# Input loads ordered tensor by tensor, weight quarters between them, two scalars loaded late, and a new list order for a gated linear attention with an MLP behind it

## The chip, the cores and the metric

The kernel runs on one core of one Trainium2 chip. The metric is the device time of one execution in microseconds (us), lower is better. TensorE (PE) multiplies matrices, VectorE (DVE) and ScalarE (ACT) work on elements, GpSimd (POOL) does a few products and casts, SyncE (SP) only issues DMAs here. Each engine takes its own instructions strictly in the order in which they were written; semaphores join the engines.

## The reference, cut to what matters

A linear attention whose state decays by `alpha` feeds a two-layer MLP with a squared relu:

```python
# q, k, v, alpha: (4 batches, 8 heads, 768 steps, 48); w_in (384, 2048), w_out (2048, 384)
for t in range(S):
    state = alpha[:, :, t, :, None] * state + einsum('bhd,bhe->bhde', k[:, :, t], v[:, :, t])
    y[:, :, t] = einsum('bhd,bhde->bhe', q[:, :, t], state)
x = y.transpose(0, 2, 1, 3).reshape(B * S, H * D)      # 3072 tokens of 384
r = maximum(x @ w_in, 0)
out = (s * (r * r) + b) @ w_out                         # s and b are single numbers
```

The kernel computes the attention in chunks. With c the running sum of log(alpha) in a chunk it forms q·exp(c) and k·exp(-c), multiplies them, masks the product to the lower triangle and multiplies it by v; what came before the chunk enters through the state.

## The kernel before

**Blocks.** The 3072 tokens are 24 blocks of 128, six to a batch. Blocks are numbered from 0. A block needs four loads of 192 KB (`a` for alpha, `q`, `k`, `v`), each into one of five buffers of its kind (`NIN = 5`). Then, per block:

- `ln` (ACT) takes the logarithm, `cum` (PE) sums it with a triangular matrix, `ei` and `eb` (ACT) take exp(-c), exp(c) and the decay over the block.
- `kb` and `qb` (DVE) multiply k and q by these; `vc` (POOL) casts v to bf16.
- q and k are transposed: in blocks below `NPE` by eight PE transposes (`T`) and a DVE copy (`Tc`), in the others by a DMA transpose that ACT issues (`Td`).
- `KV` (PE) forms the block's share of the state, `t1` (DVE) adds the old state, `sn` (POOL) applies the decay.
- `A` (PE, L404) multiplies k by q, `mk` (DVE, L413) masks, `y` (PE, L442) multiplies by v and adds the old state, `ye` (ACT, L466) copies y to bf16. From block `NAY` on, `A` of a block and `y` of the block before it are one unit of PE work, `st_Ay`; below it they are two.

**MLP.** Two blocks form a group (12 groups). A group takes eight *units* of `mm1` (L488, six matmuls of 128x256: two of the 16 slices of `w_in`), each followed by `re` (relu, ACT, L497) and `sq` (two squares, DVE, L505). It then takes eight *quads* of `mm2` (L512, four matmuls of 128x384; four quads make a block's output row), and `oe` (DVE, L523) scales by s, adds the bias and writes the tile that `ostore` (SP, L535) stores. Units and quads are counted from 0 to 95 each. Quad 4c+3 ends output c.

**Weights.** `w_in` and `w_out` come in quarters of 768 KB (`i0` to `i3`, `o0` to `o3`) through four staging buffers. ACT casts each to bf16 (`ci`, `co`; L250, L263). DVE also sums the `w_out` quarters over rows (`cp`, `ca`; L271, L276). The bias row is b times that sum: `bias_mul` (DVE, L279) makes a matrix full of b, `bias_mm` (PE, L285) multiplies it by the sums, `bias_copy` (DVE, L294) brings it to SBUF.

**What sets the order.** All of this is written down as a list of operations for a list scheduler (`Schedule`), which runs when the program is built. Each operation has an engine, a planned duration, a priority and the names it reads and writes. Per engine the scheduler takes, among the operations that could begin first by its plan, the one with the lowest priority number. The order in which it starts them is the order in which the instructions are written for each engine. Operations marked `lock` do not overlap with each other in the plan (DVE and POOL). A block's priorities are `want(n)` plus an offset in `P`; `UNIT`, `LEAD`, `P_BM`, `P_CS`, `P_BMM` and `NAY`, `NPE` shape them. `LOADS` lists the loads on SP: the scheduler sees them with priorities around -1000, so SP issues them as soon as a buffer is free, in the list's order, while stores have -2000. In the kernel before, `LOADS` holds whole blocks (`b1` means `a1 q1 k1 v1`), with the eight weight quarters between them; block 0 is issued ahead of the list, and `b` and `s` (512 bytes each after the broadcast to 128 partitions) are issued by ACT at the start. Before the first quad PE fills planned idle time with small matmuls on zeros (`fill`, L674).

Of the kernel before, what the change touches and what calls it, by code (L numbers as in the profile page):

```python
# [15 lines left out]
VW = 144  # L16

GROUPS = [2, 2, 2, 2, 2, 2, 2, 2, 2, 2, 2, 2]
UNIT = 1.396
LEAD = {1: 72.9, 2: 87.9, 4: 83.9}  # L20

NPE = 9

NAY = 5

RING = 12

NST = 4

TB = 1.1  # L30
TW = 2.3
FILL_GAP = 0.45

P_BM, P_CS, P_BMM = -5, -48.2, -221.5
P = dict(
    ln=9.85, cum=-2.97, eb=3.53, ei=-4.54, vc=-2.78, qb=15.79, kb=-10.16, T=5.42,
    Tc=-1.09, KV=4.4, t1=4.97, sn=-0.59, Ay=-5.51, A=-4.02, mk=-10.39, y=12.28,
    ye=-10.99, m1=3.02, re=-4.95, sq=-1.4, m2=14.39, oe=-25.12,
)

LOADS = ["b0", "i0", "i1", "b1", "i2", "b2", "b3", "i3", "o0", "o1", "o2", "o3", "b4", "b5", "b6"]

class Schedule:
    HOP = 0.05
# [6 lines left out]
    def op(self, eng, dur, prio, fn, *args, r=(), w=(), lat=0.08, lock=False):  # L51
        me = len(self.ops)
        deps = set()
        for x in r:
            if x in self.writer:
                deps.add(self.writer[x])
        for x in w:
            if x in self.writer:
                deps.add(self.writer[x])
            deps.update(self.readers.get(x, ()))  # L60
        for x in r:
            self.readers.setdefault(x, []).append(me)
        for x in w:
            self.writer[x] = me
            self.readers[x] = []
        self.ops.append((eng, dur, prio, fn, args, deps, lat, lock))
# [67 lines left out]
def kernel(  # L134
# [12 lines left out]
    nc = tc.nc  # L147
# [6 lines left out]
    NBLK = B * NCH  # L154
# [3 lines left out]
    NIN = 5  # L158
# [16 lines left out]
    def many(name, n, shape, dtype, zero=None):  # L175
        tiles = []
        for i in range(n):
            t = sb.tile(shape, dtype, name=f"{name}{i}")
            if zero is not None:
                zero.memset(t, 0.0)  # L180
            tiles.append(t)
        return tiles


    a_in = many("a_in", NIN, [128, H, D], FP32)
    q_in = many("q_in", NIN, [128, H, D], FP32)
    k_in = many("k_in", NIN, [128, H, D], FP32)
    v_in = many("v_in", NIN, [128, H, D], FP32)
    s_col = sb.tile([128, 1], FP32, name="s_col")
    b_col = sb.tile([128, 1], FP32, name="b_col")  # L190
# [8 lines left out]
    for src, dst in ((alpha, a_in), (q, q_in), (k, k_in), (v, v_in)):  # L199
        load(0, src, dst)  # L200
    nc.scalar.preload_act_table_set("natural_log_exp_and_others")
    nc.scalar.dma_start(out=b_col, in_=moe_b.to_broadcast((128, 1)))
    nc.scalar.dma_start(out=s_col, in_=moe_s.to_broadcast((128, 1)))

    la_sb = many("la", 2, [128, H, 64], BF16, zero=nc.vector)
    U_bf = sb.tile([128, 128], BF16, name="U_bf")
# [29 lines left out]
    bones = sb.tile([128, 128], FP32, name="bones")  # L236
# [37 lines left out]

    def colsum_add():
        nc.vector.tensor_tensor(out=colsum, in0=colsum, in1=colpart, op=ALU.add)  # L276

    def bias_mul():
        nc.vector.tensor_scalar(  # L279
            out=bones, in0=ones_f, scalar1=b_col, scalar2=None, op0=ALU.mult  # L280
        )
# [257 lines left out]
    op = sched.op  # L539
    NG = len(GROUPS)  # L540

    def first(n):
        return n % NCH == 0

    def last(n):
        return n % NCH == NCH - 1

    def want(n):
        g, t = blk_group[n]
        return (4 * n - LEAD[GROUPS[g]]) * UNIT  # L550

    loads = LOADS + [f"b{n}" for n in range(NBLK) if f"b{n}" not in LOADS]
    stage = 0
    for rank, item in enumerate(loads):
        t, i = rank - 1000, int(item[1:])
        if item[0] == "b":
            if i == 0:
                for x, name in enumerate("aqkv"):
                    op("SP", 1.4 if x == 0 else 0.85, t + 0.01 * x, lambda: None,
                       w=[(name, 0)], lat=2.0)  # L560
                op("DVE", 0.3, P_BM, bias_mul, w=["bones"], lock=True)
            continue
        st = stage % NST
        stage += 1
        if item[0] == "i":
            op("SP", TW, t, load_w_in, i, st, w=[("wst", st)], lat=2.0)
            op("ACT", 1.4, -500, cast_w_in, i, st, r=[("wst", st)], w=[("wib", i)])
        else:
            op("SP", TW, t, load_w_out, i, st, w=[("wst", st)], lat=2.0)
            op("ACT", 1.4, -400, cast_w_out, i, st, r=[("wst", st)], w=[("wob", i)])  # L570
            op("DVE", 0.88, P_CS, colsum_part, i, st, r=[("wst", st)],
               w=["colpart" if i else "colsum"], lock=True)
            if i:
                op("DVE", 0.88, P_CS, colsum_add, r=["colpart"], w=["colsum"], lock=True)
# [5 lines left out]
    def yevac_op(n):  # L580
        g = blk_group[n][0]
        op("ACT", 0.41, want(n) + P["ye"], st_yevac, n, r=["py"], w=[("xd", g % 3, blk_group[n][1])])
# [3 lines left out]
    def add_block(n):  # L586
        i2, i3, ii = n % 2, n % 3, n % NIN
        t = want(n)
        if n:
            rank = loads.index(f"b{n}") - 1000  # L590
            for x, (name, src, dst) in enumerate(
                (("a", alpha, a_in), ("q", q, q_in), ("k", k, k_in), ("v", v, v_in))
            ):
                op("SP", TB, rank + 0.1 * x, load, n, src, dst, w=[(name, ii)], lat=2.0)
        op("ACT", 0.45, t + P["ln"], st_ln, n, r=[("a", ii)], w=[("la", i2)])
        op("PE", 0.27, t + P["cum"], st_cum, n, r=[("la", i2)], w=["ct"], lat=0.16)
        op("ACT", 0.41, t + P["eb"], st_exp_b, n, r=["ct"], w=[("b", i2)])
        op("ACT", 0.49, t + P["ei"], st_exp_i, n, r=["ct"], w=[("bi", i2), ("bl", i2)])
        op("POOL", 0.5, t + P["vc"], st_vcast, n, r=[("v", ii)], w=[("vp", n % 4)], lock=True)
        op("DVE", 0.48, t + P["qb"], st_qb, n, r=[("q", ii), ("b", i2)], w=[("qb", i3)], lock=True)  # L600
        op("DVE", 0.48, t + P["kb"], st_kb, n, r=[("k", ii), ("bi", i2)], w=[("kb", i3)], lock=True)
        if n < NPE:
            op("PE", 0.45, t + P["T"], st_T, n, r=[("qb", i3), ("kb", i3)], w=["ct"], lat=0.16)
            op("DVE", 0.61, t + P["Tc"], st_Tcopy, n, r=["ct"], w=[("qkT", i3)])
        else:
            op("ACT", 1.25, t + P["T"], st_Tdma, n, r=[("qb", i3), ("kb", i3)],
               w=[("tq", i3), ("qkT", i3)], lat=0.1)
            op("SP", 1.95, -3000, lambda: None, r=[("tq", i3)], w=[("qkT", i3)], lat=2.0)
        op("PE", 0.17, t + P["KV"], st_KV, n, r=[("kb", i3), ("vp", n % 4)], w=["py"], lat=0.16)
        if first(n):  # L610
            op("DVE", 0.65, t + P["t1"], st_t1, n, r=["py", ("bl", i2)], w=[("S", i3)])
        elif not last(n):
            op("DVE", 0.65, t + P["t1"], st_t1, n, r=["py", ("S", (n - 1) % 3)], w=[("t1", i2)])
            op("POOL", 0.85, t + P["sn"], st_snew, n, r=[("t1", i2), ("bl", i2)], w=[("S", i3)], lock=True)
        rA, wA = [("qkT", i3)], ["a"]
        late = n + 1 < NBLK and n + 1 >= NAY
        if n >= NAY:
            r1, w1 = ys.pop(n - 1)
            op("PE", 0.935, want(n - 1) + P["Ay"], st_Ay, n, r=rA + r1, w=wA + w1, lat=0.16)
            yevac_op(n - 1)  # L620
        else:
            op("PE", 0.43, t + P["A"], st_A, n, r=rA, w=wA, lat=0.16)
        op("DVE", 1.14, t + P["mk"], st_mask, n, r=["a"], w=[("am", i2)])
        rr = [("am", i2), ("qkT", i3), ("vp", n % 4)] + ([] if first(n) else [("S", (n - 1) % 3)])
        if late:
            ys[n] = (rr, ["py"])
        else:
            op("PE", 0.6, t + P["y"], st_y, n, r=rr, w=["py"], lat=0.16)
            yevac_op(n)

    def add_group(g):
# [4 lines left out]
        for u in range(NJ // per):  # L636
            w = unit_i
            unit_i += 1
            js = units[w][1]
            t = w * UNIT  # L640
            op("PE", 0.85 if m == 1 else 0.65, t + P["m1"], mm1, w,
# [5 lines left out]
        for u in range(4 * m):  # L647
# [3 lines left out]
            ob = (x // 4) % 2  # L651
            t = (x + 4 * m + P["m2"]) * UNIT
            op("PE", 0.65, t, mm2, x,
# [7 lines left out]
    for n in range(NBLK):  # L661
        add_block(n)

        if n and n >= NAY and blk_group[n - 1][0] != blk_group[n][0]:
            add_group(blk_group[n - 1][0])
        if (n + 1 < NAY or n + 1 == NBLK) and n + 1 == first_blk[blk_group[n][0]] + GROUPS[blk_group[n][0]]:
            add_group(blk_group[n][0])
# [41 lines left out]
```

## Time and profile before

| what | value |
| --- | --- |
| median of 5 runs | 199.25 us (197.66 to 200.53) |
| the profiled execution's own time | 198.28 us |
| its span, first to last instruction | 196.2 us |
| TensorE clock granted in it | 1.000 |
| PE, DVE, ACT, POOL busy | 176.5, 148.1, 108.8, 33.9 us |
| loads and stores | 34.16 MB moved, 174 GB/s mean |
| filler matmuls (L674) | 58, 10.6 us |

The span leaves out 2.1 us of the execution's time that lie around the first and last instruction. Durations come from the one profiled execution. A busy PE counts filler matmuls and matmuls whose ends are modelled, so busy time is not the same as work done. Where matmuls follow one another without a gap, the time from one start to the next is the better measure: 0.65 us for a unit of `mm1` or a quad of `mm2`, 0.33 for `A`, 0.51 for `y` (0.34 in the first block of a batch), 0.27 for `cum`, 0.19 for `KV`, 0.46 for eight transposes.

### The profile page before, as it was taken

Reading aid. Unit: us, or ns where it says so; the run is one execution under the profiler, and the core shown is the slowest. Engines: PE = TensorE matmul, PEld = TensorE weight load, DVE = VectorE, ACT = ScalarE, POOL = GpSimd, SP = SyncE. Lnnn points to the kernel's source line nnn. Section 1 sums busy time; section 2 is a strip of 40 time slices with the busy share of each in tenths; the row PEclk is TensorE's granted clock in tenths of the full one; section 3 lists DMA queues with packets and bytes.
Section 4 is the critical chain, followed back from the end, with each engine's and each line's share of the span. In section 5 each row is a group of like instructions: output and inputs, shape, how many; then the busy total and the mean of one; then the engine's idle time right before and its main releaser. Section 6 shows DMA issues by size and latency. Waiting matters only on the chain.

```text
span 196.2 us, 5398 instructions
## 1 busy us (share of the span) xinstructions
PE 176.5 (90%) x2126; PEld 127.5 (65%) x2126; DVE 148.1 (75%) x353; ACT 108.8 (55%) x225; POOL 33.9 (17%) x60
## 2 busy tenths in 40 slices
PE   0688988599999899999999699999999999999992
PEld 0456766367567567777777477677676677776861
DVE  4344697799988999798977878857898889775541
ACT  3172974995235666557566467267467257355520
POOL 8401321001202123120121220301130221100000
PEclk9999999999999999999999999999999999999999
DMA  4999899977999989996699985999697899510012
GB/s 83 251 291 256 173 234 380 327 141 164 192 186 227 199 167 173 204 216 133 143 195 143 202 185 119 191 241 181 138 240 145 169 198 178 97 40 24 19 40 82
DMA packets 123161, 34.16 MB, mean 174 GB/s; under 512 B 116480, under 2 KB 121600, under 8 KB 123136
## 3 DMA queue, kind: packets, MB, share of 16 engines
q1 hardware_dynamic: 107008, 29.89, 68.9%
q10 hardware_dynamic: 16128, 3.94, 12.4%
q8 instruction: 16, 0.26, 0.6%
q14 instruction: 9, 0.07, 0.1%
HBM read 25.17 MB, written 4.72 MB: 152 GB/s over the span
## 4 chain that ended last, share of the span: by engine, by line
PE 60%; DMA 17%; DVE 15%; issue 3%; ACT 1%; SPq 1%; ACTq 0%; DVEq 0%
PE o_ps L512 24%; PE h_ps L488 22%; DMA k_in<-in_k_dram 8%; DMA wst<-in_moe_w_out_dram 5%; PE py_ps L442 4%; DVE gt L505 4%; DMA qkT<-qk 4%; PE a_ps L404 3%; DVE am L413 2%; DVE qkT L371 2%; PE o_ps L674 2%; PE ct_ps L348 2%; PE ct_ps L304 1%; DVE t L387 1%; DVE colpart L271 1%
## 5 line engine op out<-in xcount | busy, mean ns | idle before, releaser
L497 ACT ACTIVATE r<-h_ps 128x512 bf16<-128x512 f32 x96 | 55.8, 600 | 34.6 <-PE h_ps L488 19.2
L512 PE MATMUL o_ps<-w_out_bf,gt 128*128 128x384 bf16 x384 | 71.8, 326 | 2.6 <-ACT w_out_bf L263 2.6
L488 PE MATMUL h_ps<-xd,w_in_bf 128*128 128x256 bf16 x576 | 72.5, 273 | 0.6 <-ACT xd L466 0.2
L505 DVE TENSOR_TENSOR gt<-r 128x256 bf16<-128x256 bf16 x192 | 55.6, 337 | 15.7 <-ACT r L497 15.1
L488 PEld LDWEIGHTS <-w_in_bf 128*128 128x128 bf16 x576 | 54.6, 98 | 10.9 <-issue 1.2
L512 PEld LDWEIGHTS <-gt 128*128 128x128 bf16 x384 | 35.8, 98 | 22.2 <-issue 2.7
L413 DVE TENSOR_TENSOR am<-a_ps,mask 128x1024 bf16<-128x1024 f32 x24 | 29.3, 1219 | 2.0 <-PE a_ps L404 1.7
L398 POOL TENSOR_TENSOR s_st<-t,blast 128x384 bf16<-128x384 bf16 x16 | 14.6, 912 | 65.5 <-DVE t L387 37.9
L325 POOL CAST vp<-v_in 128x384 bf16<-128x384 f32 x24 | 13.9, 578 | 67.4 <-DMA v_in<-in_v_dram 53.0
L466 ACT ACTIVATE xd<-py_ps 128x384 bf16<-128x384 f32 x24 | 11.8, 490 | 22.6 <-PE py_ps L442 21.0
L523 DVE SCALAR_TENSOR_TENSOR o_sb<-o_ps,s_col,bias_w 128x384 f32<-128x384 f32 x24 | 14.8, 616 | 7.3 <-PE o_ps L512 6.5
L336 DVE TENSOR_TENSOR qk<-k_in,binv 128x384 bf16<-128x384 f32 x24 | 13.8, 577 | 8.6 <-ACT binv L321 6.5
L298 ACT ACTIVATE la<-a_in 128x384 bf16<-128x384 f32 x24 | 12.5, 522 | 5.4 <-DMA a_in<-in_alpha_dram 3.7
L321 ACT ACTIVATE binv<-ct_ps 128x384 f32<-128x384 f32 x24 | 11.8, 491 | 4.6 <-PE ct_ps L309 4.4
L331 DVE TENSOR_TENSOR qk<-q_in,b_s 128x384 bf16<-128x384 f32 x24 | 13.5, 563 | 0.3
L404 PE MATMUL a_ps<-qkT 64*128 64x128 bf16 x192 | 9.7, 222 | 4.1 <-DVE qkT L371 2.4
L318 ACT ACTIVATE b_s<-ct_ps 128x384 f32<-128x384 f32 x24 | 12.1, 505 | 1.5 <-issue 1.5
L387 DVE TENSOR_TENSOR t<-py_ps,s_st 64x192 bf16<-64x192 f32 x32 | 11.3, 353 | 2.1 <-PE py_ps L362 1.7
L304 PE MATMUL ct_ps<-la,U_bf 128*128 128x384 bf16 x24 | 8.0, 335 | 4.9 <-ACT la L298 4.8
L404 PEld LDWEIGHTS <-qkT 64*128 64x128 bf16 x192 | 5.5, 95 | 10.6 <-DVE qkT L371 4.5
L442 PE MATMUL py_ps<-am,vp 128*32 128x128 bf16 x384 | 9.8, 223 | 1.5 <-DVE am L413 1.5
L674 PE MATMUL o_ps<-zeros,ident_bf 128*128 128x256 bf16 x58 | 10.6, 333 | 0.0
(42 smaller groups left out, 107.4 us busy)
## 6 DMA issues: line engine op xcount, KB each, us to landing
a_in<-in_alpha_dram SPq DMA_DIRECT2D x24, 192.0 KB, 4.1
q_in<-in_q_dram SPq DMA_DIRECT2D x24, 192.0 KB, 3.9
k_in<-in_k_dram SPq DMA_DIRECT2D x24, 192.0 KB, 4.4
v_in<-in_v_dram SPq DMA_DIRECT2D x24, 192.0 KB, 4.2
out_dram<-o_sb SPq DMA_DIRECT2D x24, 192.0 KB, 2.1
wst<-in_moe_w_in_dram SPq DMA_DIRECT2D x4, 768.0 KB, 6.4
wst<-in_moe_w_out_dram SPq DMA_DIRECT2D x4, 768.0 KB, 10.0
qkT<-qk ACTq DMA_TRANSPOSE x15, 4.6
```

The source lines that it names most:

```text
L325: nc.gpsimd.tensor_copy(out=vp_sb[n % 4].rearrange("a p (x d) -> a p x d", d=D)[:, :, 0:3:2, :], in_=v_in[n % NIN].rearrange("a (p e) d -> ...
L336: nc.vector.tensor_tensor(out=qk_sb[n % 3][:, 1, :, 0:D], in0=k_in[n % NIN], in1=binv_sb[n % 2], op=ALU.mult,)
L398: nc.gpsimd.tensor_tensor(out=s_sb[n % 3], in0=t1_sb[n % 2], in1=bl, op=ALU.mult)
L404: nc.tensor.matmul(out=a_ps[:, e, p, :], lhsT=qkT[64 * e : 64 * e + 64, 1, p, :], rhs=qkT[64 * e : 64 * e + 64, 0, p, :], start=True, stop ...
L413: nc.vector.tensor_tensor(out=am_sb[n % 2].rearrange("a e p t -> a (e p) t"), in0=a_ps.rearrange("a e p t -> a (e p) t"), in1=mask.unsquee ...
L442: nc.tensor.matmul(out=y_ps[32 * (x % 4) : 32 * (x % 4) + 32, x // 4, :], lhsT=(st[:, p, c0 : c0 + 32] if e is None else vp[:, p, c0 + 48 ...
L488: nc.tensor.matmul(out=hp[:, i * n : (i + 1) * n], lhsT=w_in_bf[:, kk, 128 * j : 128 * (j + 1)], rhs=xd_sb[g % 3][:, kk, 0:n], start=(kk = ...
L497: nc.scalar.activation(out=r_sb[w % 2], in_=h_ps[w % 2], func=AF.Relu)
L505: nc.vector.tensor_tensor(out=gt_sb[j][:, c0 : c0 + n], in0=r, in1=r, op=ALU.mult)
L512: nc.tensor.matmul(out=op[:, 0:d_model], lhsT=gt_sb[j][:, c0 : c0 + C], rhs=w_out_bf[:, j, :], start=(j == 0), stop=(j == NJ - 1),)
L523: nc.vector.scalar_tensor_tensor(out=ots, in0=o_ps[(x // 4) % 2][:, 0:d_model], scalar=s_col, in1=bias_w, op0=ALU.mult, op1=ALU.add,)
L674: nc.tensor.matmul(out=o_ps[0][:, 0:256], lhsT=ident_bf, rhs=zeros[:, 0:256], start=True, stop=True)
```

## The change

`LOADS` no longer names blocks but single tensors, and the weight quarters stand among the tensors of blocks 1 to 3. After block 0 SP issued

- before: `i0 i1 | a1 q1 k1 v1 | i2 | a2 q2 k2 v2 | a3 q3 k3 v3 | i3 o0 o1 o2 o3 | a4 q4 k4 v4`
- now: `v1 a1 k1 q1 | i0 | a2 k2 | i1 | q2 a3 q3 | i2 | v2 k3 | i3 | v3 | o0 o1 o2 o3 | a4 q4 | b s | k4 v4`

The two scalars leave ACT's queue and go through SP, behind `q4`; `bias_mul` now reads `b` by name in the list and so is placed later on DVE. Three empty operations at the head of the list stand for the start-up work of POOL, DVE and ACT in the plan. The planned durations of loads, `UNIT`, `LEAD`, all offsets of `P`, `NPE` (9 to 8) and `NAY` (5 to 9) are new, so the order changes on every engine through the whole kernel. The mathematics and the tiles are the same; one block more (16 in place of 15) is transposed by DMA.

```diff
-UNIT = 1.396
-LEAD = {1: 72.9, 2: 87.9, 4: 83.9}
-NPE = 9
-NAY = 5
+UNIT = 1.163
+LEAD = {1: 88.8, 2: 82.1, 4: 260.5}
+NPE = 8
+NAY = 9
-TB = 1.1
-TW = 2.3
+TB = 1.02
+TW = 2.15
-P_BM, P_CS, P_BMM = -5, -48.2, -221.5
+P_BM, P_CS, P_BMM = -5, 415.9, 233.9
 P = dict(
-    ln=9.85, cum=-2.97, eb=3.53, ei=-4.54, vc=-2.78, qb=15.79, kb=-10.16, T=5.42,
-    Tc=-1.09, KV=4.4, t1=4.97, sn=-0.59, Ay=-5.51, A=-4.02, mk=-10.39, y=12.28,
-    ye=-10.99, m1=3.02, re=-4.95, sq=-1.4, m2=14.39, oe=-25.12,
+    ln=-17.34, cum=53.58, eb=-33.14, ei=-46.37, vc=-50.13, qb=33.16, kb=15.39, T=-45.58,
+    Tc=13.15, KV=-44.58, t1=18.38, sn=-7.17, Ay=83.04, A=33.34, mk=12.7, y=25.87,
+    ye=17.29, m1=-28.55, re=40.52, sq=7.1, m2=61.85, oe=-32.76,
 )
-LOADS = ["b0", "i0", "i1", "b1", "i2", "b2", "b3", "i3", "o0", "o1", "o2", "o3", "b4", "b5", "b6"]
+LOADS = ["v1", "a1", "k1", "q1", "i0", "a2", "k2", "i1", "q2", "a3", "q3", "i2", "v2", "k3", "i3", "v3", "o0", "o1", "o2", "o3", "a4", "q4", "z0", "k4", "v4"]
...
-    nc.scalar.dma_start(out=b_col, in_=moe_b.to_broadcast((128, 1)))
-    nc.scalar.dma_start(out=s_col, in_=moe_s.to_broadcast((128, 1)))
...
+    def load_bs():
+        nc.sync.dma_start(out=b_col, in_=moe_b.to_broadcast((128, 1)))
+        nc.sync.dma_start(out=s_col, in_=moe_s.to_broadcast((128, 1)))
...
-    loads = LOADS + [f"b{n}" for n in range(NBLK) if f"b{n}" not in LOADS]
+    op("POOL", 5.6, -9000, lambda: None)
+    op("DVE", 3.4, -9000, lambda: None)
+    op("ACT", 2.2, -9000, lambda: None)
+    SRC = {"a": (alpha, a_in), "q": (q, q_in), "k": (k, k_in), "v": (v, v_in)}
+    loads = list(LOADS)
+    for n in range(1, NBLK):
+        loads += [f"{x}{n}" for x in "aqkv" if f"{x}{n}" not in LOADS]
+
+    def load_op(x, n):
+        op("SP", TB, loads.index(f"{x}{n}") - 1000, load, n, *SRC[x], w=[(x, n % NIN)], lat=2.0)
...
-                op("DVE", 0.3, P_BM, bias_mul, w=["bones"], lock=True)
+        if item[0] == "z":
+            op("SP", 0.6, t, load_bs, w=["b", "s"], lat=2.3)
+            op("DVE", 0.3, P_BM, bias_mul, r=["b"], w=["bones"], lock=True)
```

More of the change, by code (lines that the diff above doesn't have):

```diff
@@ L550, in want @@
         return (4 * n - LEAD[GROUPS[g]]) * UNIT
-    loads = LOADS + [f"b{n}" for n in range(NBLK) if f"b{n}" not in LOADS]
+    op("POOL", 5.6, -9000, lambda: None)
[7 more added lines that the diff above has]
+        op("SP", TB, loads.index(f"{x}{n}") - 1000, load, n, *SRC[x], w=[(x, n % NIN)], lat=2.0)
     stage = 0
+    for x in range(4):
+        op("SP", 1.4 if x == 0 else 0.85, -2000 + x, lambda: None, w=[("aqkv"[x], 0)], lat=2.0)
     for rank, item in enumerate(loads):
         t, i = rank - 1000, int(item[1:])
[L556 to L560, printed above, removed]
-                op("DVE", 0.3, P_BM, bias_mul, w=["bones"], lock=True)
+        if item[0] in "aqkv":
+            if i < NIN:
+                load_op(item[0], i)
+            continue
+        if item[0] == "z":
+            op("SP", 0.6, t, load_bs, w=["b", "s"], lat=2.3)
+            op("DVE", 0.3, P_BM, bias_mul, r=["b"], w=["bones"], lock=True)
             continue
@@ L588, in add_block @@
         t = want(n)
[L589 to L594, printed above, removed]
+        if n >= NIN:
+            for x in "aqkv":
+                load_op(x, n)
         op("ACT", 0.45, t + P["ln"], st_ln, n, r=[("a", ii)], w=[("la", i2)])
```

## The prediction

> **What bounds the kernel now.** I read the page for engine shares first, then the windows by stage, the chain of waits in order of time, and the timelines of DVE and POOL where the chain leaves PE.
>
> ```profile
> PE 176.5 (90%) x2126; PEld 127.5 (65%) x2126; DVE 148.1 (75%) x353; ACT 108.8 (55%) x225; POOL 33.9 (17%) x60
> PE   0688988599999899999999699999999999999992
> DMA  4999899977999989996699985999697899510012
> ```
>
> PE is the busy engine, but 10.6 of its 176.5 us are filler. So I count the work instead, with the start-to-start times of unbroken runs: 96 units at 0.655, 96 quads at 0.65, 24 x `A` 0.33, `y` 20 x 0.51 and 4 x 0.34, `cum` 24 x 0.27, `KV` 24 x 0.19, nine blocks' transposes at 0.46, the bias matmuls 1.46: 161.4 us. The span is 196.2, so PE lacks work for 34.8 us. Where? I place each `A` by the work ahead of it in PE's order and subtract that from its start in the trace.
>
> | PE reaches | starts at | work ahead | lost so far |
> | --- | --- | --- | --- |
> | A of block 4 | 48.3 | 23.0 | 25.3 |
> | A of block 7 | 65.0 | 37.5 | 27.5 |
> | A of block 11 | 90.4 | 62.2 | 28.2 |
> | A of block 14 | 110.5 | 80.3 | 30.2 |
> | end of the last quad | 192.7 | 161.4 | 31.3 |
>
> After that the last output's scaling and store take 3.5. The loss thus lies in the front (25.3), between blocks 4 and 8 (about 2.7), at block 14 (1.8), and little elsewhere.
>
> ```profile
> 20.00:30.00 10.00, 8.22 (x131) 6.17 (x128) 8.22 (x18) 8.18 (x17) 2.95 (x4) 1.00 0.96 221
> 30.00:40.00 10.00, 7.42 (x93) 5.65 (x94) 7.87 (x18) 7.30 (x9) 0.83 (x1) 1.00 1.02 331
> 40.00:50.00 10.00, 9.55 (x85) 6.64 (x84) 9.87 (x25) 7.99 (x17) 1.85 (x3) 1.00 0.78 159
> 60.00:65.00 5.00, 3.81 (x48) 3.14 (x41) 4.49 (x9) 3.30 (x8) 1.58 (x3) 1.00 1.09 230
> 65.00:70.00 5.00, 4.99 (x69) 3.98 (x70) 4.96 (x13) 3.30 (x8) 0.93 (x2) 1.00 0.87 171
> ```
>
> Columns: window, PE, PEld, DVE, ACT, POOL busy, clock, DMA share, GB/s. Up to 40 us the DMA engines are full; from 40 to 50 it is DVE (9.87 of 10) and ACT; from 60 to 70 DVE again (9.45 of 10).
>
> ```profile
> 21.64 0.50 ACT xd L466
> 22.18 1.47 PE h_ps L488 x12
> ...
> 25.59 10.78 DMA wst<-in_moe_w_out_dram
> 36.40 0.96 DVE colpart L271
> ...
> 95.81 0.62 DVE o_sb L523
> 96.43 0.21 DVE gt L505
> 96.87 0.43 SPq L194
> 97.34 4.85 DMA k_in<-in_k_dram
> 102.22 0.75 DVE qk L336
> 103.00 7.42 DMA qkT<-qk
> 110.46 0.40 PE a_ps L404 x8
> ```
>
> The chain of waits shows both ends: the front hangs on `w_out` arriving, and block 14 on k, which SP issued only after a store that waited for its `oe`: 14.65 us from that `oe` to `A`.
>
> ```profile
> 63.11 1.12 DVE L505 TENSOR_TENSOR gt<-r 128x256 bf16<-128x256 bf16 x2
> 63.25 0.83 POOL L398 TENSOR_TENSOR s_st<-t,blast 128x384 bf16<-128x384 bf16 x1 [2.85 <-DVE t L387]
> ```
>
> The timelines of DVE and POOL (start, duration): two squares on DVE last 1.12 us while POOL forms a state product.
>
> **What the Trainium skill says.** *DMA: Bandwidth & Descriptors*, section "Why small descriptors are slow", charges each small descriptor a fixed overhead: order cannot shorten what must arrive. The trace agrees: 192 GB/s or so while blocks of 192-byte pieces come, 380 GB/s in the slice of `w_out`. *SBUF — State Buffer*, "SBUF: two separate sides", makes the port of DVE and POOL an exclusive lock. The trace agrees: a pair of squares takes 0.41 to 0.48, but 1.12 at 48.67, 63.11 and 69.11, each beside a state product of POOL of 0.84.
>
> **Front, to 34 us.** The new order brings `v1 a1 k1 q1` right behind block 0. From the landings of before (k1 at 15.1; four tensors about 4.3 us, a weight quarter about 2.75) they land at 8.7 to 11.9, and i0 at 14.7. Block 1's `y` ends near 16.5, the first unit starts near 17 (before: 22.18). But i1, i2, i3 now come later, about 19.6, 25.5 and 30.4, and units 2, 4 and 6 wait for their casts (1.48 each). Block 3 ends its `y` at 34.2 in my walk; before 34.3. Ahead of o0 the same twelve block tensors beyond block 0 and four quarters must come, over DMA engines that were full in both, so o0 stays at 34.3. Gain so far: 0.
>
> **34 to 48 us.** Both orders run units 8 to 15 and quads 0 to 3 between the four `co` casts. The new order has one relu (unit 6) ahead of o0 rather than behind it, 0.55 less for ACT; DVE gets `bias_mul` 0.29 behind the last sum. Behind that on DVE are a square and `kb`, `qb` of block 4, and PE's bias matmuls. b is issued after q4 (landed 41.97), about 42.3 if it keeps its place; `bias_mul` comes to its turn at 44.2, so b is hidden, with 2 us of cover. PE then has the same eight pieces up to `A` of block 4. I take 48.0 (48.3): loss 25.0.
>
> **Blocks 4 to 11.** PE's new order (m1 unit, m2 quad):
>
> ```
> A4 cum5 m2.5-7 y4 m2.8 T5 KV5 m2.9-10 A5 cum6 m2.11-12 y5 m2.13 T6 KV6 m1.16-17 A6 cum7
> m1.18-19 y6 m2.14 m1.20 T7 KV7 m1.21-22 A7 cum8 m1.23 m2.15 y7 cum9 m2.16 KV8 m1.24 m2.17-19
> cum10 KV9 m1.25-26 m2.20-21 A8 m1.27-28 cum11 m2.22-24 A9 y8 m1.29-30 KV10 m2.25 m1.31
> m2.26 A10 y9 m2.27
> ```
>
> I walk it with the durations of before (`mk` 1.22, `kb` and `qb` 0.55, squares 0.48 a pair or 1.12 beside POOL, `Tc` 0.69, `t1` 0.73, `oe` 0.62, `re` 0.60, `ei` and `eb` 0.5).
>
> - Better: transposes of block 7 have 3.0 us of PE work behind `cum` (before 1.5), and 1.5 instead of 1.3 between them and `A`. A7 comes at 64.6 with 39.2 of work ahead: lost 25.4, where before it was 27.5.
> - Worse: up to block 8, `y` waits for its own mask, with 1.6 us of work in between (before 4.4 to 5.5). The mask needs about 1.45 with its hops, so it just fits, unless DVE is late.
> - Worse: quad 19 needs the squares of unit 23. Unit 23 ends at 65.9, but its relu stands on ACT behind `ei8 eb8 ye7`, the DMA transpose (1.25), `ei9 eb9 ln10`: it ends at 71.0, the squares at 71.8; PE arrives at 70.4. Loss 1.45. Behind quad 19 wait `cum10`, and so `kb10`.
> - Worse: quads 26 and 27 wait for squares that stand behind `t1` (with a POOL product) and behind the mask of block 10: 84.15 against 83.1, and 86.8 against 85.65: 1.05 and 1.15.
>
> Sum at block 11: 25.4 + 0.45 (y7 and small ones) + 1.45 + 1.05 + 1.15 = 29.5, before 28.2. So the 2.1 gained is paid back with 1.3 on top.
>
> **Block 14.** Its q and k again stand behind the store of output 7. From quad 31's end to `A14` there are 14.2 us of PE work, before 12.9. Against the measured 14.65, and 0.4 for `qb14` now behind `kb14`, 0.85 is left of a stall of 1.8. Loss at block 14: 30.35, before 30.2.
>
> **Rest.** The other loads behind stores have 13.0 us of work up to their `A` or more, before 13.5 or more, and in the trace those of 13.5 to 13.7 did not stall. From unit to quad the later blocks have 3.3 us or more, before down to 1.8, without stalls. I keep the 1.1 of before, and 3.5 at the end. One block fewer is transposed on PE: 0.46 less work (and 0.69 less of DVE); the DMA transpose that replaces it has 8.6 us between `cum8` and `A8`, plus the stall at quad 19, against latencies of 3.1 to 7.4: hidden.
>
> Sum: 160.9 + 30.35 + 1.1 + 3.5 = 195.9, before 196.2. That is 0.3 less; on the median (1.0 above the profiled execution) 198.9. A measurement here tells about 1% (2 us) from nothing.
>
> **Rivals.**
> - *The DVE stalls don't come.* Back to back, DVE's instructions start closer than they last (kb to qb 0.47), so my walk may hold DVE too long. Without the 3.65 of quads 19, 26 and 27: 195.2. For it: before, PE lost nothing between 75 and 100 us with DVE at 4.7 of 5. Against it: quad 19's wait is ACT's order, not DVE's speed.
> - *The front shrinks.* The first unit's 5 us earlier carries through, say half: 196.4. Against it: every quad waits for `w_out`, which no order brings sooner.
> - *Slower: masks late in blocks 4 to 8.* Each `y` waits directly for its mask on a DVE that is full. If DVE is 0.7 late (one POOL collision) at five blocks, PE loses 3.5, as nothing else stands before `y`: 202.4. It decides if masks start over 0.3 after the end of their `A`.
> - *Slower: b comes late.* It has no row in SP's queue. Bounds: 0 (cover 2 us), and, if it takes q4's whole 8.9 us from an issue at 37 to 38, landing at 46.5: `bias_mul` 2.3 late, DVE's queue with it: 201.2. I take 0.
>
> **How the numbers follow.** No measurable change 0.43; DVE stalls absent 0.23 and shorter front 0.10, together faster 0.33; late masks 0.17 and late b 0.07, together slower 0.24. The range reaches from just under 195.2 to just over 202.4: 194.6 to 202.8. The likeliest case alone holds 197.3 to 200.9.
>
> **What would show it.** First unit near 17 us; o0's cast still at 34 to 35; `A4` at 48; quad 19 idle before it, released by DVE's square; stall at A14 below 1 us. It is wrong if `A4` comes before 46 or after 50, if PE idles before `y` in blocks 4 to 8, or if `bias_mul` waits on a DMA.

## The result, and the profile after

The change makes no difference that the measurements here can tell. The changed kernel was measured three times, each time beside the kernel before; none of the three ratios is 1% away from 1, and they do not agree on a direction:

| measurement | median after / before (us) | ratio, 95% interval |
| --- | --- | --- |
| first | 198.45 / 197.73 | 0.9913 [0.9876, 0.995] |
| `e1_new_again` | 198.81 / 197.76 | 1.005 [1.0004, 1.0095] |
| `e11_new_third` | 199.84 / 197.96 | 0.9976 [0.9933, 1.0019] |

The medians are over all executions, but a ratio compares only those within 1.5% of each kernel's own fastest (6 of 44, 9 of 12 and 6 of 22 for the changed kernel), so for a kernel that scatters widely it looks better than the quotient of the medians, which is 1.004, 1.005 and 1.009 here. The first profile of the changed kernel has a lowered clock (0.991 on the mean), and the profile of `e1_new_again` stands here for the kernel after. Its span is 195.4 us (before 196.2), its own time 197.18.

```profile
PE 176.3 (90%) x2105; PEld 125.8 (64%) x2105; DVE 147.6 (76%) x352; ACT 107.8 (55%) x225; POOL 33.4 (17%) x60
PE   1859977789999999999999999978999989999992
DMA  6999999959979999898899999879998993801112
```

Shares and slices hardly differ from before. The loss of PE, counted as in the prediction (start of `A` less the work ahead of it in PE's own order), does differ, by place:

| lost up to | before | `e1_new_again` | `e11_new_third` | first profile |
| --- | --- | --- | --- | --- |
| A4 | 25.3 | 23.6 | 23.5 | 22.9 |
| A7 | 27.5 | 24.9 | 25.1 | 24.0 |
| A11 | 28.2 | 25.8 | 25.9 | 24.8 |
| A14 | 30.2 | 26.1 | 26.2 | 25.7 |
| A17 | 30.4 | 26.9 | 26.6 | 26.5 |
| A18 | 30.5 | 29.2 | 28.2 | 28.2 |
| A21 | 30.7 | 29.6 | 29.5 | 29.2 |
| A23 | 31.0 | 30.6 | 32.3 | 33.8 |
| span | 196.2 | 195.4 | 197.1 | 198.6 |

By block 17 the new kernel is 3.5 to 3.9 us ahead. After it, it gives back 3.1, 5.1 and 6.7 us more than the kernel before loses there. The windows by stage (PE, PEld, DVE, ACT, POOL busy, clock, DMA share, GB/s) of `e1_new_again`, with the last window of the kernel before below them:

```profile
20.00:30.00 10.00, 8.05 (x117) 6.30 (x114) 7.90 (x19) 8.54 (x13) 2.19 (x3) 1.00 0.95 276
30.00:40.00 10.00, 8.20 (x93) 6.23 (x90) 9.35 (x21) 8.25 (x11) 0.84 (x1) 1.00 0.94 297
40.00:50.00 10.00, 9.13 (x101) 5.90 (x100) 9.24 (x20) 6.26 (x16) 1.85 (x3) 1.00 0.87 169
60.00:65.00 5.00, 4.90 (x69) 3.61 (x67) 4.51 (x14) 3.98 (x10) 1.26 (x2) 1.00 1.06 208
65.00:70.00 5.00, 4.92 (x65) 3.28 (x64) 4.92 (x12) 3.08 (x10) 0.75 (x3) 1.00 0.98 190
120.00:135.00 15.00, 13.56 (x173) 9.71 (x172) 10.07 (x27) 8.81 (x22) 1.24 (x3) 1.00 0.89 166
```

```profile
120.00:135.00 15.00, 15.00 (x212) 10.58 (x210) 10.09 (x29) 8.27 (x19) 2.22 (x3) 1.00 1.04 205
```

In 30 to 40 us PE is busy 0.78 us more than before, in 60 to 65 1.09 more. The last window holds the new hole: 1.44 us without PE work, where the kernel before had none. The timeline of `e1_new_again` there (start, duration, engine, operation, in brackets the idle time before it and its releaser):

```profile
121.88 0.62 DVE L525 SCALAR_TENSOR_TENSOR o_sb<-o_ps,s_col,bias_w 128x384 f32<-128x384 f32 x1
...
122.53 0.36 SPq L537 DMA_DIRECT2D out_dram<-o_sb  x1
122.94 0.44 SPq L194 DMA_DIRECT2D k_in<-in_k_dram  x1
...
128.79 0.56 DVE L338 TENSOR_TENSOR qk<-k_in,binv 128x384 bf16<-128x384 f32 x1 [2.12 <-ACT r L499]
...
129.27 0.55 DVE L333 TENSOR_TENSOR qk<-q_in,b_s 128x384 bf16<-128x384 f32 x1
...
129.85 1.29 ACTq L355 DMA_TRANSPOSE qkT<-qk  x1
...
131.27 1.09 ACT L499 ACTIVATE r<-h_ps 128x512 bf16<-128x512 f32 x2 [3.31 <-DVE gt L507]
...
131.92 1.47 PE L490 MATMUL h_ps<-xd,w_in_bf 128*128 128x256 bf16 x12 [1.44 <-ACT r L499]
```

Read it downwards as one chain. The `oe` of output 11 ends at 122.5; its store was first in SP's queue and had waited for it; only then can SP issue k of block 18, which lands at 128.7. Meanwhile DVE stands before `kb18` and ACT before the DMA transpose of block 18. Behind that transpose in ACT's queue are relus whose inputs are ready; the tiles that they write to come free with squares that stand behind `kb18` on DVE. PE runs out of free buffers for its units and waits for a relu. The releasers in brackets name the last step or a nearby one; the start of the chain is a store.

The kernel before has this chain too, with the same links (the store of output 11 ahead of k of block 18, that block's transpose ahead of two relus), and got through it:

```profile
124.64 0.62 DVE L523 SCALAR_TENSOR_TENSOR o_sb<-o_ps,s_col,bias_w 128x384 f32<-128x384 f32 x1
...
126.18 0.69 SPq L194 DMA_DIRECT2D k_in<-in_k_dram  x1
...
130.92 0.56 DVE L336 TENSOR_TENSOR qk<-k_in,binv 128x384 bf16<-128x384 f32 x1 [0.32 <-ACT b_s L318]
...
133.40 1.09 ACT L497 ACTIVATE r<-h_ps 128x512 bf16<-128x512 f32 x2 [1.51 <-PE h_ps L488]
```

In both lists PE has 10.0 us of work between the last quad of output 11 and the unit that needs the first of these relus. In the kernel before that quad ends at 124.37 and the relu ends 9.62 us later; in `e1_new_again` the quad ends at 120.42 and the relu 11.45 us later. Two things account for the difference. The new list puts `kb17` and `qb17` ahead of the `oe`, which starts 1.46 us after its quad (before 0.27), and k takes 5.8 us from issue to landing (before 4.7). Half a us is won back, as q now goes out ahead of the store.

### The profile page after: what moved, and what is told of

It reads as the page before. It is cut to its first block, busy times and chain, and to the rows that moved or that the text cites. A ratio compares the mean times of both kernels' runs of the same rounds, so it can differ in the third digit from the quotient of the medians.

```text
span 198.6 us, 5369 instructions
## 1 busy us (share of the span) xinstructions
PE 177.2 (89%) x2105; PEld 126.2 (64%) x2105; DVE 148.6 (75%) x352; ACT 107.8 (54%) x225; POOL 33.0 (17%) x60
## 4 chain that ended last, share of the span: by engine, by line
PE 52%; DVE 14%; SPq 13%; issue 6%; ACT 6%; DMA 5%; ACTq 2%; DVEq 0%
PE h_ps L490 22%; PE o_ps L514 21%; SPq L194 9%; DVE gt L507 5%; ACT r L499 4%; DMA wst<-in_moe_w_in_dram 3%; PE py_ps L444 3%; DVE am L415 2%; DVE qk L333 2%; PE a_ps L406 2%; DMA k_in<-in_k_dram 2%; SPq L277 2%; SPq L240 2%; PE py_ps L364 1%; ACTq L355 1%
## 5 line engine op out<-in xcount | busy, mean ns | idle before, releaser
L400 POOL TENSOR_TENSOR s_st<-t,blast 128x384 bf16<-128x384 bf16 x16 | 14.0, 874 | 54.5 <-DVE t L389 40.1
L333 DVE TENSOR_TENSOR qk<-q_in,b_s 128x384 bf16<-128x384 f32 x24 | 15.0, 627 | 0.3 <-ACT b_s L320 0.3
L364 PE MATMUL py_ps<-vp,qk 128*128 128x96 bf16 x96 | 8.6, 215 | 1.0 <-ACT xd L468 1.0
```

The source lines that it names most:

```text
L333: nc.vector.tensor_tensor(out=qk_sb[n % 3][:, 0, :, 0:D], in0=q_in[n % NIN], in1=b_sb[n % 2], op=ALU.mult)
L400: nc.gpsimd.tensor_tensor(out=s_sb[n % 3], in0=t1_sb[n % 2], in1=bl, op=ALU.mult)
```

## The experiments

All ratios are to the kernel before, run on the same chip.

**The changed kernel again, and with the scalars early.** `e1_new_again` is the changed kernel. `e2_new_scalars_early` gives the two scalars back to ACT at the start and leaves all orders as they are:

```diff
+    nc.scalar.dma_start(out=b_col, in_=moe_b.to_broadcast((128, 1)))
+    nc.scalar.dma_start(out=s_col, in_=moe_s.to_broadcast((128, 1)))
...
-            op("SP", 0.6, t, load_bs, w=["b", "s"], lat=2.3)
+            op("SP", 0.6, t, lambda: None, w=["b", "s"], lat=2.3)
```

> The changed kernel once more, to see which of its marks hold from execution to execution. If the shorter front is a property of the order, the first w_out quarter lands again near 30.5 us and A of block 4 starts near 45.9 us (before: 34.3 and 48.3). If it was chance, these fall between the two. If the wait ahead of block 22 (relu behind a DMA transpose that waits for kb and qb, 4.5 us lost between A of block 21 and A of block 22) belongs to the order, it is there again; if it came from the throttled execution, it is under 1 us and the end lies near 193 us.

> The changed kernel with only one thing undone: b and s are loaded by ACT at the start as before; everything else keeps its place. Theory 'scalars': two DMAs of 128 pieces of 4 bytes among the first loads slow block 0. Then k0 lands near 7.0 us in place of 5.7, A of block 0 starts near 10.0 in place of 8.7, and the first w_out quarter lands 1 to 4 us later than in the changed kernel. Theory 'load order': nothing changes by more than 0.3 us.

Measured: 1.005 [1.0004, 1.0095] and 0.9999 [0.9953, 1.0044]. With the scalars early, k of block 0 lands at 7.1 us rather than 5.6, and the first quarter of `w_out` at 32.9 rather than 31.5. But k of block 4 lands 1.8 us *earlier*, at 41.5 rather than 43.4, since b and s no longer stand ahead of it. The chain of waits of `e1_new_again` shows this (start, duration; L277 and L278 issue b and s):

```profile
30.79 4.65 SPq L194
35.48 3.36 SPq L277
38.88 0.59 SPq L278
39.52 3.84 DMA k_in<-in_k_dram
...
43.93 0.55 DVE qk L333
```

Both kernels lose 23.6 us up to A4. So in these two executions it made no difference to PE where the scalars stand: the change moves a delay of 1.5 us ahead of block 0 to one of 1.8 us ahead of k of block 4.

**The load order alone, on each list.** `e3_new_block_loads` keeps the new list order of PE, DVE, ACT and POOL but loads blocks 1 to 3 by whole blocks; `e5_old_strewn_loads` puts the strewn loads under the old list order.

```diff
+    FIRST = ['i0', 'i1', 'a1', 'q1', 'k1', 'v1', 'i2', ...]   # e3; e5: 'v1', 'a1', 'k1', 'q1', 'i0', ...
+    def fix(begin):                       # after the list is planned, SP's first 16 loads alone
+        for x, o in enumerate(sched.ops):
+            ...
+                begin[x] = -100 + 0.01 * FIRST.index(...)
```

> The changed kernel with the first 16 loads of SP in the order of before (i0 i1, block 1, i2, block 2, block 3, i3); b and s stay late, all other engines keep the new order. Theory 'load order': the first w_out quarter lands at 34 us again, the front is 2.4 us or more longer, the whole 1 to 2% slower than the changed kernel. Theory 'scalars': it still lands near 31 to 32. In both the first unit of the MLP starts later (block 1 lands at 15 to 16 us).

> The kernel before with only SP's first 16 loads put into the new order (v1 a1 k1 q1 i0 a2 k2 i1 ...); scalars early and all other engines as before. Theory 'the load order shortens the front by itself': A of block 4 starts 1 us or more before 48.3, and the time falls by about 1%. Theory 'the load order pays only with the new order on ACT and PE' (the old order casts i0 and i1 before it takes the logarithm of block 1): no gain, A of block 4 at 48 to 50, the time 0 to 1% longer. If DMA engines move the strewn order faster, the first w_out quarter lands before 33 us.

Measured: 1.0131 [1.0073, 1.019] and 1.0266 [1.0222, 1.0309]. The loss up to A4 is 25.9 and 29.8. Half of the change, in either combination, is slower than none of it; each was measured with four executions. In `e5_old_strewn_loads` the reason is in ACT's timeline: the old order has the casts of `i0` and `i1` ahead of the logarithm of block 1, and those quarters now come later.

```profile
14.45 1.48 ACT L254 ACTIVATE w_in_bf<-wst 128x1536 bf16<-128x1536 f32 x1 [8.10 <-DMA wst<-in_moe_w_in_dram]
...
18.39 1.48 ACT L254 ACTIVATE w_in_bf<-wst 128x1536 bf16<-128x1536 f32 x1 [2.09 <-DMA wst<-in_moe_w_in_dram]
19.78 0.51 ACT L302 ACTIVATE la<-a_in 128x384 bf16<-128x384 f32 x1
```

ACT waits 8.10 us with a cast at its head while block 1 already lies in SBUF. Under the new list the strewn order does save time at the front: 23.6 us are lost up to A4 in `e1_new_again`, 25.9 in `e3_new_block_loads`. The order of loads needs a list order written for it.

**The late scalars alone, on the old list.** `e4_old_scalars_late` takes nothing else from the change:

```diff
+        if n == 4 and src is q:
+            nc.sync.dma_start(out=b_col, in_=moe_b.to_broadcast((128, 1)))
+            nc.sync.dma_start(out=s_col, in_=moe_s.to_broadcast((128, 1)))
...
+            if o[3] is bias_mul:
+                begin[x] = at + 1e-6      # behind the square of unit 11
```

> The kernel before with only the scalars moved: b and s on SP behind q4, and the multiplication by b put behind the squares of unit 11 on DVE, where the change has it. Theory 'scalars': block 0 lands 1.3 us earlier, the first w_out quarter near 31 to 33, A of block 4 near 46 to 47, and the time falls by 0.5 to 1.2%. Theory 'load order': the quarter still lands near 34, the time is within 0.3% of before.

Measured: 0.9971 [0.9942, 1.0]. The loss up to A4 is 24.4, before 25.3. The first `w_out` quarter lands 1.4 us sooner, k of block 4 0.8 later. This is no gain that the measurement tells from none.

**What takes the gain back.** Two theories for the stretch behind block 17: the store ahead of the loads on SP, or the DMA transpose ahead of the relus on ACT. `e6_new_stores_behind` puts each store on SP directly behind the next load of v, and changes no other engine; `e7_new_transposes_behind` puts a DMA transpose behind the one or two relus that directly follow it on ACT; `e8_new_both` does both.

```diff
+        vs = sorted(begin[x] for x, o in enumerate(sched.ops) if o[3] is load and o[4][1] is v)
...
+            if o[3] is ostore:                              # e6, e8
+                nxt = [t for t in vs if t > begin[x]]
+                begin[x] = nxt[0] + 1e-6
...
+            if sched.ops[x][3] is st_Tdma:                  # e7, e8
+                while r < p + 2 and sched.ops[act[r + 1][1]][3] is relu: r += 1
+                begin[x] = act[r][0] + (1e-6 if r > p else 0)
```

> The changed kernel with only SP's order altered: each store waits behind the four loads of the block in which it stood, so no q or k load waits for a store. Theory 'stores ahead of loads' (the store waits for its output, k lands late, kb and qb are late, the DMA transpose on ACT waits for them and holds the relus behind it): the losses between A17 and A18 (2.3 us) and between A21 and A22 (0.8 to 4.5) fall below 0.5 each, PE no longer waits for relus there, the span is 192 to 193 and the median 1 to 2% under the changed kernel. Theory 'ACT's order alone' or 'throttled clock': both losses stay.

> The changed kernel with only ACT's order altered: seven or so DMA transposes that stand directly ahead of one or two relus are issued behind these. k lands as late as before. Theory 'the held relus are what costs': PE's waits for relus at blocks 18 and 22 vanish, and as the transpose itself goes out at the same time, the span is 193 to 194. Theory 'late k costs anyway': the loss moves to A of blocks 18 and 22, which then wait for the transposed tiles, and the span stays at 195 to 196.

> The changed kernel with both: stores behind the loads and transposes behind the relus. If late loads are the cause, this is no better than stores behind loads alone (within 0.5 us of its span). If each removes a part, it is 1 us better than either.

Measured: 0.9835 [0.9761, 0.991], 1.0103 [1.0045, 1.0161] and 1.0053 [1.0024, 1.0082]. With the stores behind, the loss from A17 to A23 is 1.6 us (24.8 to 26.4), where `e1_new_again` has 3.7. The same stretch in the timeline and the windows of `e6_new_stores_behind`:

```profile
124.52 0.55 DVE L342 TENSOR_TENSOR qk<-k_in,binv 128x384 bf16<-128x384 f32 x1
...
125.56 1.25 ACTq L359 DMA_TRANSPOSE qkT<-qk  x1
...
126.99 1.25 ACT L503 ACTIVATE r<-h_ps 128x512 bf16<-128x512 f32 x2 [1.11 <-PE h_ps L494]
...
128.33 1.48 PE L494 MATMUL h_ps<-xd,w_in_bf 128*128 128x256 bf16 x12
```

```profile
120.00:135.00 15.00, 15.00 (x206) 10.59 (x204) 11.68 (x28) 8.08 (x19) 1.02 (x2) 1.00 0.96 183
```

`kb18` runs 4.3 us earlier (2.1 of it because this execution had lost 2.1 less by A17), the relus now wait for PE instead of the other way round, and PE is busy all 15.00 us. Moving the transposes instead does not free the relu at block 18: it starts at 131.40, 1.54 us after `kb18`, since its tile comes free with squares behind `kb18`. And the transposed tile can come late for its `A`. In `e7_new_transposes_behind` PE's timeline has, at block 11:

```profile
88.55 0.40 PE L410 MATMUL a_ps<-qkT 64*128 64x128 bf16 x8 [2.12 <-DMA qkT<-qk]
```

`e8_new_both` has no wait for a relu of 0.15 us or more, but three `A` wait 4.2 us together for transposed tiles; I had expected its span within 0.5 us of that of `e6_new_stores_behind`, and it is 197.5 against 191.1. So on the new list the relu is where the stall is met, and the store ahead of the load is what makes it. It is a near thing: `e2_new_scalars_early` and `e3_new_block_loads`, with the stores ahead too, lose only 0.1 us between A17 and A18 (their k of block 18 landed 4.0 and 3.7 us after its issue), but 1.9 and 3.8 between A21 and A22.

**Repeats and the same edit on the old list.** `e10_new_stores_behind_again` repeats `e6_new_stores_behind`, `e11_new_third` the changed kernel; `e9_old_stores_behind` makes the SP edit in the kernel before, and `e12_old_scalars_late_stores_behind` adds the late scalars to that.

> The kernel before with only SP's order altered: each store behind the four loads of its block; scalars early, loads by blocks. Theory 'the old order had the room that the new one lacks': only the stall ahead of A of block 14 (1.8 us of 30.2 lost) goes, the median falls by 0.5 to 1%. Theory 'stores ahead of loads cost the same in both': the gain is as large as in the changed kernel, 1.6 to 2%.

> The changed kernel with stores behind the loads, once more and with more rounds, beside the changed kernel itself on the same chip. If the gain holds, it is 1.2 to 2% faster than before, the span 191 to 193.5, with under 0.5 us lost between A17 and A18 and between A21 and A22. If the first look was lucky, it is within 1% of before.

> The changed kernel a third time, with more rounds. If what the two looks so far show holds, it is within 1% of before on either side (0.995 to 1.008), and the front's loss up to A of block 4 is 22.9 to 23.6 us again. Theory 'the gain is given back late': 1.5 us or more are lost between A17 and A23.

> The kernel before with the scalars late and the stores behind the loads; order of loads and of all other engines as before. If the new load order and list order have a worth of their own, this stays 2 us or more behind the changed kernel with stores behind loads: a span near 193.5 to 194.5, 1 to 1.5% faster than before, with 24.4 us lost up to A of block 4. If they have none, it reaches 191 to 192.

Measured: 1.0016 [0.9979, 1.0054], 0.9856 [0.9813, 0.9898], 0.9976 [0.9933, 1.0019] and 1.0001 [0.997, 1.0032]. The gain of the SP edit on the new list is repeated (from A17 to A23 the second execution loses 1.5 us, 26.6 to 28.1), and it is the best version found: median 195.23 in the first and 194.86 in the second measurement, beside 197.49 and 197.96 before. On the old list it brings nothing, with the scalars late either: the old kernel has only 0.6 us of loss behind A17 to win. The new orders thus have a worth of their own once the stores are out of the way: median 194.86 against 198.35 in `e12_old_scalars_late_stores_behind`. At block 14 of `e9_old_stores_behind` `A` still waited 1.23 us for its transposed tile, and my expectation that this stall would go was wrong. Its trace shows why. k of block 14 now lands at 98.0 (before 102.2), but `kb14` starts at the same time as before (102.22), in its turn on DVE:

```profile
102.25 1.18 DVE L340 TENSOR_TENSOR qk<-k_in,binv 128x384 bf16<-128x384 f32 x1
```

The transpose is issued at 103.47 (before 103.00) and its tile lands 7.1 us later (before 7.4). In `e12_old_scalars_late_stores_behind` it is issued at 103.26, lands after 5.7 us, and `A` does not wait. So at block 14 the store was not what made the stall; why that transpose takes so long is open.

## Why the prediction was right, and where its steps were not

The forecast of no measurable change (198.9, range 194.6 to 202.8) holds, but three of its steps were wrong. That they cancelled is luck: in two the new kernel did better than forecast, in one worse. By one of its own signs (A4 before 46) the first profile, with A4 at 45.86, even spoke against it.

- **Front, "o0 stays at 34.3. Gain so far: 0": failed.** The `w_out` quarter landed at 30.5, 31.5 and 31.0 in the three executions. I had compared bytes and left out that the scalars leave the stretch before it. They account for about 1.4 us (`e1_new_again` against `e2_new_scalars_early`, and `e4_old_scalars_late` against before), give or take the 1.8 us by which o0 scatters over the seven traces with the changed kernel's front (30.0 to 31.8). The rest, 1.3 us in `e2_new_scalars_early` (32.9 against 34.3), comes with the new order of loads and list: with block loads under the new list o0 came at 31.4 and with strewn loads under the old one at 32.4, so order can bring it sooner, and how the rest divides stays open. The first unit started at 18.4 (predicted 17). The loss up to A4 is 22.9 to 23.6, predicted 25.0. The rival of a shrinking front was right in its direction and, at 1.7 to 2.4 us by A4 against the 2.5 that its half of 5 us meant, near in size; its time did not come, because of what follows late.
- **34 to 48 us, "b is hidden": held, but I stopped there.** b lands at 41.1, 0.8 behind q of block 4, and `bias_mul` runs at 42.2 without a wait. What I did not count is that b and s also stand ahead of k of block 4: the gap from q4 to k4 grew from 0.8 to 3.1 us, and `kb4` waited 0.60 for it.
- **Blocks 4 to 11: the gain at A7 came, the stalls at quads 19, 26 and 27 did not.** A4 to A7 costs 1.3 (before 2.2). A7 to A11 costs 0.9; I had 4.1 there (25.4 to 29.5). In 45 to 85 us the waits of PE in `e1_new_again` name no other engine at all. So this step put 3.2 us too much into the sum. It failed in the count of quads. I read the 20th quad in PE's order as quad 19, but two outputs alternate there (16, 17, 18, 20, 19, 21 ... 24, 25, 28, 26, 29, 27), so the 20th is the first quad of the next output and needs units 16 and 17, not 23. The squares of unit 23 ran at 71.31, and PE had gone from 68.63 to 70.58 through quads without needing them. The rival "the DVE stalls don't come" was right about the fact, for another reason than the spacing of DVE's instructions that it gave.
- **Masks late (rival): fell.** From A4 to A8 PE lost 1.7 us (before 2.7); no `y` waited 0.3 us or more for its mask.
- **Block 14, "0.85 is left of a stall of 1.8": right in direction, too large by size.** 0.3 us were lost from A11 to A14 in `e1_new_again`, 0.4 in `e11_new_third`, 0.9 in the first profile. The reading behind it was wrong in part: before, `kb14` waited only 0.35 us for k, and taking the store away did not remove the stall (`e9_old_stores_behind`).
- **Rest, "loads behind stores have 13.0 us of work up to their `A` or more": failed.** This is the step that hides the largest miss: I kept 1.1 us for everything behind block 14, and 3.7 to 7.3 came between A17 and A23 alone. The distance to `A` was nearly enough: in the three traces one `A` behind block 14 waits, that of block 18 in `e1_new_again`, 0.55 us. But `A` is not what is met first. Between the landing of k and `A` stand `kb` on DVE and the DMA transpose on ACT, and *behind these* in the same queues stand squares and relus that PE needs sooner: 10.0 us of work away from the last quad of output 11, where the chain took 11.45. Both lists have the transposes of blocks 18 and 22 ahead of such relus; before, the chain took 9.62 at block 18, and the new list spent that room.

The sum for `e1_new_again` against before, in us: front −1.7, A4 to A11 −0.7, A11 to A17 −1.1, A17 to A23 +3.1, the end +0.1, less PE work −0.5: together −0.8, which is the 196.2 less 195.4 of the spans. The changed kernel's executions scatter more than before's (198.45 with 193.81 to 201.93 in the first measurement, 197.73 with 196.18 to 200.53 before), and the three profiles differ most behind block 21, where the same chain comes at block 22: PE waited 0.72 there in `e1_new_again`, 2.49 in `e11_new_third` and 2.80 in the first profile, where a lower clock behind that wait adds to it. k of block 22 took 4.5, 5.3 and 5.9 us to land in these three, and the issue of the transpose 1.25, 2.32 and 2.08.

The clock goes with the scatter as well. In 49 of the 78 executions of the changed kernel the mean granted clock was below 0.995, in 13 of the 98 of the kernel before in the second and third measurement; the medians of the changed kernel's executions below and above that lie 1.9 to 2.2 us apart. In the first profile the mean of 0.991 is one stretch of 3.4 us at half clock. How much of the scatter is the chain and how much the clock, and whether the chain's waits bring the lower clock about, is not shown. Without the stores ahead (`e6_new_stores_behind`, `e10_new_stores_behind_again`) the clock was below 0.995 in 2 of 10 executions, and all ten lie between 192.90 and 196.59.

## What to carry to other kernels

When a load stands behind a store in one queue, do not ask only how far off its final consumer is: follow the load through each queue it will block, and find the first instruction behind it that the bottleneck engine needs. Begin the count at the work that fills the stored tile, and allow for what stands ahead of that work in its own queue. An order of loads and the order of the engines' work are one thing; half of a joint re-ordering cost 1.3% and 2.7% here, where the whole made no difference that could be measured. And where several outputs are accumulated at once, read which output an instruction belongs to before you count it by its position.

## What the hardware showed that I had not expected

- Two loads of 128 pieces of 4 bytes are not small: from the landing of q4 to that of k4 it takes 3.0 to 4.5 us in the ten traces that have them between, 0.7 to 1.0 in the four that do not. And k of block 0 lands at 6.9 to 7.2 us in the four traces that have them early, at 5.3 to 5.9 in the ten others.
- A DMA transpose that waits for its input holds all of ACT (3.31 us between two relus at block 18 of `e1_new_again`, its own issue included). Its issue takes 1.25 us of ACT's queue in most cases, and up to 2.1 us in `e1_new_again` and 2.3 in `e11_new_third`.
- A load of 192 KB has no fixed time to land. k of block 18 took 3.7 us from issue to landing in `e3_new_block_loads` and 5.9 in the first profile, and behind it PE did not wait in the one and waited 1.55 us in the other.
- In the first profile the granted clock fell to 0.50 from 161.8 to 165.2 us, just behind PE's wait of 2.80 us that ended at 160.8. In `e11_new_third` it stayed at 1.00 behind a wait of 2.49 at the same place, so whether the wait caused it is open.
